# Head-pair groups outermost, K and attention outputs transposed by DMA, half-row score matmuls adjoining, output projection summed per group in SBUF

## The chip, the core and the metric

The kernel runs on one core of one Trainium2 chip. The metric is the device time of one execution in microseconds (us); lower is better. The kernel before took 1077.17 us, the median of 3 runs (1077.12 to 1077.2).

An execution can be profiled. The profile gives the "span" of that one execution, which is about 1.8 us shorter than the time of the same execution (957.5 and 959.26 us in the changed kernel), and for each engine when it was busy and what it waited for. TensorE is named PE (its weight loads PEld), VectorE DVE, ScalarE ACT, GpSimd POOL, and SyncE SP. In the kernels, tiles with `_ps` in their name lie in PSUM, where the results of matmuls are summed; the other tiles lie in SBUF, and DVE or ACT copies from one to the other.

## The reference

A layer norm of x (2048 rows, 640 columns) feeds two branches that are multiplied and added to x. All data is bf16.

```python
xn = layernorm(x)                                   # 2048 x 640
# branch A: 32 heads of 192, only the last W = 512 keys of the cache
q  = (xn @ wq).reshape(2048, 32, 192)
p  = softmax(q @ k_cache[:, -512:].T * 192 ** -0.5)
A  = (p @ v_cache[:, -512:]).reshape(2048, 6144) @ wo
# branch B: a gated feed-forward
B  = (sigmoid(xn @ w_gate) * (xn @ w_up)) @ w_down  # inner width 1536
out = x + A * silu(B)
```

## The kernel before

It has two parts. The feed-forward part (phase B) computes silu(B) for all rows and parks it in memory. The attention part (phase A) takes blocks of 512 rows, `s`, outermost. Inside it goes through the 16 pairs of heads. A head has 192 columns, so a pair has three chunks of 128: one chunk for each head, and one that holds 64 columns of both. The first two give full-row matmuls (all 128 rows of the array contracted), the shared one gives half-row matmuls (64 rows), one head in the upper and one in the lower half.

```python
def stage1(st, hp, pair_idx):            # for each (s, pair)
    # ... loads K, V and wq of the pair again for every s; q projection ...
    for c in range(KC):                  # KC = 4: twelve transposes of K on TensorE
        for i in range(2):
            nc.tensor.transpose(kA_ps[:, i, c * P:(c + 1) * P],
                                kt[:, cb + colA[i]:cb + colA[i] + P], ident[:])
        nc.tensor.transpose(kB_ps[:, c * P:(c + 1) * P],
                            kt[:, cb + KPAD + P:cb + KPAD + 2 * P], ident[:])
    # ... copies kA_ps, kB_ps to kTA (DVE), kTB (ACT) ...

def stage_qk(st, ctxd):
    for c0 in range(0, KC, CG):          # CG = 2
        for c in cs:                     # four full-row matmuls
            for i in range(2):
                nc.tensor.matmul(S_ps[(c, i)][:], lhsT=kA[...], rhs=qA_[:], start=True, stop=False)
        for c in cs:                     # four half-row matmuls
            for i in range(2):
                nc.tensor.matmul(S_ps[(c, i)][:], lhsT=kB[...], rhs=qB_, start=False, stop=True)
        # ... exp on ACT ...

def phase_a2(st):                        # once after all 16 pairs of a block s
    for q in range(TQ):                  # 128 rows
        for fq in range(NG):             # 12 groups of 4 chunks
            for j in range(4):
                nc.tensor.transpose(pT[:, j, :], o_st[q][:, cc * P:(cc + 1) * P], ident[:])
            # copy to oT: DVE on even fq, ACT on odd fq
            for j in range(4):
                for (d0, dsz), oA_ps in zip(d_chunks, oA):
                    nc.tensor.matmul(oA_ps[:], lhsT=oT[:, j, :], rhs=wo_sb[:, cc, d0:d0 + dsz], ...)
        # ... times silu(B), plus x, store ...

for s in range(NST):                     # 4 blocks of rows
    for hp in range(NPAIR):              # 16 pairs
        ...
```

The softmax here doesn't subtract the row's maximum and nothing guards it: scores larger than these inputs give would overflow.

## Time and profile before

| | before |
|---|---|
| time, us (median) | 1077.17 |
| span of the profiled execution, us | 1071.9 |
| TensorE busy | 97% of the span |
| phase B ends (first q matmul of attention) | 177.4 us |
| one step (512 rows, one pair), 64 of them | 9.64 us |
| output phase after 16 steps, 4 of them | about 67.7 us |
| tail after the last matmul | 4.4 us |
| read from memory | 106.04 MB |

First, lines of the profile's page of the kernel before: the span, the busy time and share of each engine, and the chain of work that ended last.

```profile
span 1071.9 us, 19547 instructions
...
PE 1034.7 (97%) x7927; PEld 608.0 (57%) x8048; DVE 439.9 (41%) x1163; ACT 515.0 (48%) x981; POOL 113.9 (11%) x163
...
PE 82%; issue 10%; DMA 3%; ACT 2%; POOL 2%; DVE 1%; POOLq 0%; DVEq 0%
```

TensorE is the limit, and nothing else is near it. So work that leaves TensorE shortens the kernel, and work given to another engine or to the DMA engines costs nothing as long as it stays under TensorE's own time and is done before TensorE needs it.

The next lines are the TensorE timeline of the kernel before, in one step. The columns are start (us), duration (us), engine, line of the kernel, operation with its output and inputs, shape, and count; in brackets, where TensorE was idle before the line, how long and who released it. Matmuls are pipelined, so the distance between two starts is the cost, not the duration.

```profile
251.59 0.28 PE L254 MATMUL kA_ps<-ident,k_sb 128*128 128x128 bf16 x2
251.71 0.22 PE L258 MATMUL kB_ps<-ident,k_sb 128*128 128x128 bf16 x1
...
252.26 0.38 PE L286 MATMUL S_ps<-qT_2577,kTA 128*128 128x512 bf16 x1
...
252.69 0.38 PE L286 MATMUL S_ps<-qT_2577,kTA 128*128 128x512 bf16 x1
252.91 0.38 PE L286 MATMUL S_ps<-qT_2593,kTA 128*128 128x512 bf16 x1
253.22 0.60 PE L293 MATMUL S_ps<-qT_2585,kTB 64*128 64x512 bf16 x4
253.76 0.39 PE L286 MATMUL S_ps<-qT_2577,kTA 128*128 128x512 bf16 x1
...
344.80 0.38 PE L343 MATMUL pTo<-ident,o_st 128*128 128x128 bf16 x4
345.74 0.39 PE L352 MATMUL oA_ps_4061<-wo_sb,oT 128*128 128x512 bf16 x1 [0.56 <-DVE oT L346]
```

Three costs are to be read from it. The twelve K transposes take from 251.59 to 252.26, 0.67 us in each of 64 steps, 0.056 us each. A full-row matmul follows a full-row one after 0.22 us, but the first half-row one comes 0.31 us after the last full one: about 0.1 us more at the switch; and four half-row ones, which run in pairs and would need two times 0.216 us, take 0.54 us (253.22 to 253.76): again 0.1 us more. Two entries and two exits in a step. And the output phase starts with a wait for the copy of its first transposes; such waits for a copy out of PSUM are called bubbles below.

### The profile page before, as it was taken

How to read it: one execution, taken by the hardware profiler on the slowest of the kernel's cores; microseconds unless marked ns; L12 is line 12 of the kernel's file. 1: busy time of each engine (PE TensorE's matmuls, PEld its weight loads, DVE VectorE, ACT ScalarE, POOL GpSimd, SP SyncE). 2: the span in 40 equal slices, each digit the busy share in tenths (PEclk: the TensorE clock that was granted, in tenths of full speed). 3: DMA queues.
4: the chain of work that ended last, by engine and by line, in shares of the span. 5: the costliest groups of instructions: out<-in, count | busy, mean ns of one | idle time of the engine just before them, and what ended most of it. 6: DMA issues, size and time to landing. Idle time of an engine off the chain costs nothing.

```text
span 1071.9 us, 19547 instructions
## 1 busy us (share of the span) xinstructions
PE 1034.7 (97%) x7927; PEld 608.0 (57%) x8048; DVE 439.9 (41%) x1163; ACT 515.0 (48%) x981; POOL 113.9 (11%) x163
## 2 busy tenths in 40 slices
PE   6899999999999999999999999999999999999997
PEld 3445445556556665656556555656566555656664
DVE  4654333444454123544452224544432244544322
ACT  2654223666656114666653235666641165666321
POOL 4211002400010001000010010000000010000000
PEclk9999999999999999999999999999999999999999
DMA  9621002975555013555552024555521054451010
GB/s 303 196 93 50 13 37 77 343 205 130 135 127 163 20 38 78 133 144 131 137 144 65 20 71 127 129 144 132 136 70 38 20 147 127 129 144 50 1 38 13
DMA packets 153578, 115.18 MB, mean 107 GB/s; under 512 B 138000, under 2 KB 140560, under 8 KB 153488
## 3 DMA queue, kind: packets, MB, share of 16 engines
q1 hardware_dynamic: 138048, 53.63, 20.3%
q0 software_dynamic: 15440, 60.30, 18.8%
q8 instruction: 63, 1.03, 0.4%
q14 instruction: 27, 0.22, 0.1%
HBM read 106.04 MB, written 7.86 MB: 106 GB/s over the span
## 4 chain that ended last, share of the span: by engine, by line
PE 82%; issue 10%; DMA 3%; ACT 2%; POOL 2%; DVE 1%; POOLq 0%; DVEq 0%
PE q_ps L236 18%; PE o_ps L315 17%; PE S_ps L286 11%; PE S_ps L293 6%; PE kA_ps L254 3%; ACT oT L348 2%; PE pTo L343 2%; DMA xnT_d<-xnT_sb 1%; PE kB_ps L258 1%; PE g_ps L160 1%; PE u_ps L167 1%; PE oA_ps_4443 L352 1%; PE oA_ps_10299 L352 1%; PE oA_ps_13091 L352 1%; PE oA_ps_7371 L352 1%
## 5 line engine op out<-in xcount | busy, mean ns | idle before, releaser
L236 PE MATMUL q_ps<-xnT_a,wqp 128*128 128x512 bf16 x901 | 214.9, 379 | 5.4 <-DMA wqp<-in_A_wq_dram 2.2
L352 PEld LDWEIGHTS <-oT 128*128 128x128 bf16 x1536 | 115.3, 98 | 102.4 <-DVE oT L346 11.8
L328 DVE TENSOR_SCALAR o_st<-o_ps,rden 128x192 bf16<-128x192 f32 x384 | 148.3, 415 | 9.0
L348 ACT ACTIVATE oT<-pTo 128x512 bf16<-128x512 bf16 x96 | 53.8, 595 | 203.2 <-PE pTo L343 203.2
L236 PEld LDWEIGHTS <-wqp 128*128 128x128 bf16 x960 | 92.4, 97 | 100.8 <-DMA wqp<-in_A_wq_dram 2.7
L321 DVE RECIPROCAL rden<-o_ps 128x2 f32<-128x2 f32 x256 | 41.6, 162 | 192.9 <-PE o_ps L315 192.9
L346 DVE COPY oT<-pTo 128x512 bf16<-128x512 bf16 x96 | 40.7, 424 | 178.5 <-PE pTo L343 177.9
L228 POOL DMA_DIRECT2D wqp<-in_A_wq_dram x64 | 55.9, 874 | 472.5 <-PE q_ps L236 428.2
L326 ACT ACTIVATE o_st<-o_ps,rden 128x192 bf16<-128x192 f32 x128 | 54.0, 422 | 66.1 <-DVE o_st L328 61.2
L286 PEld LDWEIGHTS <-kTA 128*128 128x128 bf16 x512 | 42.1, 97 | 57.4 <-issue 26.7
L265 ACT ACTIVATE kTB<-kB_ps 128x512 bf16<-128x512 bf16 x64 | 38.2, 597 | 70.1 <-PE kB_ps L258 70.1
L160 PE MATMUL g_ps<-xnT_sb,wg_sb 128*128 128x512 bf16 x236 | 62.3, 384 | 1.8 <-DVE xnT_sb L154 1.3
L167 PE MATMUL u_ps<-xnT_sb,wu_sb 128*128 128x512 bf16 x233 | 60.8, 382 | 0.2
L173 ACT ACTIVATE sig_sb<-g_ps 128x512 bf16<-128x512 f32 x48 | 28.1, 597 | 60.9 <-PE g_ps L160 60.4
L174 DVE TENSOR_TENSOR hT_sb<-u_ps,sig_sb 128x512 bf16<-128x512 f32 x48 | 32.9, 690 | 53.8 <-PE u_ps L167 44.4
L343 PE MATMUL pTo<-ident,o_st 128*128 128x128 bf16 x768 | 54.0, 219 | 0.0
L254 PEld LDWEIGHTS <-k_sb 128*128 128x128 bf16 x512 | 42.0, 98 | 15.1
L343 PEld LDWEIGHTS <-o_st 128*128 128x128 bf16 x768 | 45.8, 98 | 7.6
L254 PE MATMUL kA_ps<-ident,k_sb 128*128 128x128 bf16 x512 | 49.7, 219 | 0.0
L258 PE MATMUL kB_ps<-ident,k_sb 128*128 128x128 bf16 x256 | 46.2, 219 | 0.0
L293 PEld LDWEIGHTS <-kTB 64*128 64x128 bf16 x512 | 14.6, 94 | 54.2 <-issue 54.2
L180 PEld LDWEIGHTS <-hT_sb 128*128 128x128 bf16 x384 | 29.8, 98 | 26.7 <-DVE hT_sb L174 3.5
(1006 smaller groups left out, 1839.0 us busy)
## 6 DMA issues: line engine op xcount, KB each, us to landing
wqp<-in_A_wq_dram POOLq DMA_DIRECT2D x64, 480.0 KB, 4.6
k_sb<-in_A_k_cache_dram SPq DMA_DIRECT2D x128, 192.0 KB, 4.8
wo_sb<-in_A_wo_dram POOLq DMA_DIRECT2D x16, 480.0 KB, 9.7
v_sb_96<-in_A_v_cache_dram SPq DMA_DIRECT2D x22, 192.0 KB, 2.9
v_sb_98<-in_A_v_cache_dram SPq DMA_DIRECT2D x22, 192.0 KB, 2.9
v_sb_100<-in_A_v_cache_dram SPq DMA_DIRECT2D x21, 192.0 KB, 2.9
v_sb_102<-in_A_v_cache_dram SPq DMA_DIRECT2D x21, 192.0 KB, 2.9
v_sb_104<-in_A_v_cache_dram SPq DMA_DIRECT2D x21, 192.0 KB, 2.9
```

Of the source, the lines that this page charges most:

```text
L160: nc.tensor.matmul(g_ps[:], lhsT=wg_sb[:, c, f * P:(f + 1) * P], rhs=xnT_sb[:, c * 512:(c + 1) * 512], start=(c == 0), stop=(c == NCD - 1),)
L167: nc.tensor.matmul(u_ps[:], lhsT=wu_sb[:, c, f * P:(f + 1) * P], rhs=xnT_sb[:, c * 512:(c + 1) * 512], start=(c == 0), stop=(c == NCD - 1),)
L236: nc.tensor.matmul(q_ps[:], lhsT=wqp[:, c, j * P:(j + 1) * P], rhs=xnT_sb[:, c * 512:(c + 1) * 512], start=(c == 0), stop=(c == NCD - 1),)
L254: nc.tensor.transpose(kA_ps[:, i, c * P:(c + 1) * P], kt[:, cb + colA[i]:cb + colA[i] + P], ident[:],)
L258: nc.tensor.transpose(kB_ps[:, c * P:(c + 1) * P], kt[:, cb + KPAD + P:cb + KPAD + 2 * P], ident[:],)
L286: nc.tensor.matmul(S_ps[(c, i)][:], lhsT=kA[:, c * P:(c + 1) * P], rhs=qA_[:], start=True, stop=False,)
L293: nc.tensor.matmul(S_ps[(c, i)][:], lhsT=kB[:, c * P:(c + 1) * P], rhs=qB_, start=False, stop=True,)
L315: nc.tensor.matmul(o_ps[:, ii, 0:DH + 1], lhsT=E[i][:, c, q * P:(q + 1) * P], rhs=vt[:, c, 0:DH + 1], start=(c == 0), stop=(c == KC - 1),)
L328: nc.vector.tensor_scalar_mul(dst, o_ps[:, ii, 0:DH], rden[:, ii:ii + 1])
L343: nc.tensor.transpose(pT[:, j, :], o_st[q][:, cc * P:(cc + 1) * P], ident[:])
L348: nc.scalar.activation(oT[:], pT[:], AF.Copy)
L352: nc.tensor.matmul(oA_ps[:], lhsT=oT[:, j, :], rhs=wo_sb[:, cc, d0:d0 + dsz], start=(cc == 0), stop=(cc == NC_O - 1),)
```

## The change

The intent is to take everything but real matmuls off TensorE.

1. Groups of two head pairs are the outermost loop, and the blocks of rows run inside it. K, V and wq of a pair are then loaded and K is transposed once, not once for each of 4 blocks. The output projection of a group is added to a sum in SBUF (f32, by DVE).
2. K and the attention outputs are transposed by the DMA engines, issued on the SP queue: one DMA for each pair (K), one for each step (outputs).
3. The second half of the scores takes the half-row matmuls first, so that all eight half-row matmuls of a step adjoin: two switches in a step where there were four.
4. Phase B transposes only the first 512 rows of xn on TensorE; the rest goes by DMA, once, and stays in SBUF for attention.

The core of the diff, with cuts marked:

```diff
-        for c in range(KC):
-            # [cut] K transposes on TensorE, copies to kTA and kTB
+        kT = kt_pool.tile([P, KC * PC, P], BF16, name="kT")
+        nc.sync.dma_start_transpose(kT[:], k_sb[:].rearrange("p j e d -> p (j e d)"))
 # [cut]
+        u0 = units(range(0, KC // 2))
+        for u in u0:
+            full(*u, True)
+        for u in u0:
+            half(*u, False)
+        exps(u0)
+        u1 = units(range(KC // 2, KC))
+        for u in u1:
+            half(*u, True)
+        for u in u1:
+            full(*u, False)
+        exps(u1)
 # [cut] stage_pv, end:
+        oT = oT_pool.tile([P, TQ * PC, P], BF16, name="oT")
+        nc.sync.dma_start_transpose(oT[:], o_st[:].rearrange("p q d -> p (q d)"))
 # [cut] stage_wo, 12 matmuls for 128 rows of one group, then:
+            if g == 0:
+                nc.vector.tensor_copy(a, oA_ps[:])
+            else:
+                nc.vector.tensor_tensor(a, oA_ps[:], a, ALU.add)
+        if last:
+            nc.vector.tensor_tensor(acc[t][:], acc[t][:], gB_sb[:], ALU.mult)
+            nc.vector.tensor_tensor(o_sb[:], acc[t][:], x_sb[:], ALU.add)
 # [cut] the loop:
+    steps = [(g, s, hp) for g in range(NG) for s in range(NST) for hp in range(g * G, (g + 1) * G)]
+    for k, (g, s, hp) in enumerate(steps):
+        E = stage_s(hp, qT)
+        for _ in range(TQ // G):
+            if wo_queue and wo_queue[0][0] <= k:
+                stage_wo(*wo_queue.pop(0)[1:])
+        qT = stage_q(...)                  # of the next step
+        oT_of[hp] = stage_pv(hp, E)
+        # after a group's last pair: wo_queue.append((k + 2, g, s, oTs, q)) for each 128 rows
 # [cut] phase B:
+                nc.sync.dma_start_transpose(xnT[s][:, :, q * P:(q + 1) * P], xn[:])
```

A transposed output is used no earlier than the second step after its own, so it has a step's time and more to land.

## The prediction

> **What bounds the kernel now.** TensorE. The engine table gives it 1034.7 us busy of a 1071.9 us span (97%), DVE 41%, ACT 48% and a granted clock of 0.999; the chain of waits is 82% TensorE. So only TensorE work and its gaps count. From the timeline: phase B ends at 177.4 us; then 64 pair steps of 9.64 us each (q projection 15 x 0.216 = 3.24, K transposes 12 x 0.055 = 0.66, scores 3.01, PV 2.73), and per 512 rows an output phase of about 67.7 us (16.9 us for each 128 rows).
>
> **What the change removes from TensorE.**
> - 768 K transposes: 64 x 0.66 = 42 us.
> - 768 transposes of attention outputs, 48 x 0.055 = 2.65 us per 128 rows with bubbles around their PSUM copies: 16.9 us shrinks to the matmuls, 48 x (0.216+0.055) = 13.0. Together 16 x 3.9 = 62 us.
> - Score switches. Four full-row matmuls plus four half-row ones should take 0.87 + 0.43 us (halves run in pairs; the trace shows four in 0.54 us) but take 1.50: about 0.1 us at each entry to and exit from half rows. Four such switches per step become two: 0.2 us x 64 = 13 us.
> - Phase B: 60 of 80 x transposes with their copies and the trip of xn through DRAM (about 3 x 1.6 us), the 2.9 us wait for hT, and the 2.2 us wait for wq at the start of A: about 7 to 9 us.
>
> **What it adds.** One DMA transpose of 384 KB per step and one per pair for K, 80 in all, on the SP queue. The trace of before has none, so this is an estimate: at the 261 GB/s that the skill's "DMA: Bandwidth & Descriptors" (section "Latency and other measured facts") gives, 1.5 us plus 2 us fixed. An output is needed two steps later, about 15 us after its issue, and the queue has 9.6 us per transpose, so I expect it hidden. DVE gains 16 f32 additions per 128 rows (0.69 + 0.29 us each group), about 6.3 us per step; ACT about 5.5 us. Both are under the step. The second half of the scores waits for PSUM banks of PV just evicted by DVE: about 1.3 us needed, 1.5 available. The tail is longer: the last rows each need about 2.6 us of DVE, then the store, 11 us after the last matmul against 4.5.
>
> **Sum.** Phase B ends near 171. A step is 3.24 + 2.81 + 2.73 + two output groups of 1.63 = 12.03 us; 64 make 770. Tail 11, start of A 2, small waits 6: span 960, plus the 5 us between span and measured time: about 964 us. Range 945 to 1000. Faster 0.89, same 0.04, slower 0.07.
>
> **What the profile would show.** Right: no K or output transposes on TensorE, step period 12.0 to 12.2 us, TensorE 96% or more, DMA transposes landing in under 10 us, no long TensorE wait for oT or kT; eight half-row matmuls in about 0.97 us. Wrong on switches: eight still with gaps between.
>
> **What would make it wrong.** DMA transposes far slower than the estimate: above 9.6 us each the SP queue becomes the limit and the kernel could be slower than before. In phase B slow transposes hold the four xn buffers, which stall DVE and TensorE. PSUM waits for exp or DVE inside a step, if each reaches 0.5 us, add 30 us.

## The result

| | before | after |
|---|---|---|
| time, us, median (range, runs) | 1077.14 (1075.22 to 1077.2, 4) | 960.89 (959.26 to 963.77, 4) |
| span of the profiled execution, us | 1071.9 | 957.5 |
| TensorE busy | 97% | 97% |
| phase B ends, us | 177.4 | 176.8 |
| one step, us | 9.64 | 12.02 (holds a share of the output projection) |
| attention stage, us | 890.2 | 771.1 |
| tail after the last matmul, us | 4.4 | 9.6 |
| read from memory, MB | 106.04 | 42.07 |

The ratio of the times is 0.8936, 95% interval 0.8916 to 0.8957. Ratios here are the mean time of one kernel's fast runs over the mean of the other's in the same rounds, so not quite the ratio of the medians that are quoted.

"Attention stage" is from the start of the first q matmul to the end of the last matmul, read from the TensorE timeline of the profiled execution. It is the measure that the experiments below lean on, because phase B varied between executions and the attention stage did not.

The page of the changed kernel, the same lines:

```profile
span 957.5 us, 15630 instructions
...
PE 931.4 (97%) x6452; PEld 529.5 (55%) x6452; DVE 464.0 (48%) x1089; ACT 345.5 (36%) x668; POOL 103.1 (11%) x151
...
PE 92%; DMA 6%; DVE 1%; issue 0%; SPq 0%; POOL 0%; ACT 0%; DVEq 0%; POOLq 0%
```

TensorE lost 103 us of busy time (1034.7 to 931.4), and the span lost 114. So the rest of the gain, about 11 us, is idle time that went. The TensorE timeline of the changed kernel:

```profile
501.61 3.40 PE L273 MATMUL q_ps<-xnT_88,wqp 128*128 128x512 bf16 x15
...
513.63 3.40 PE L273 MATMUL q_ps<-xnT_88,wqp 128*128 128x512 bf16 x15
...
520.02 0.38 PE L290 MATMUL S_ps<-qT_5680,kT 128*128 128x512 bf16 x1
520.23 0.38 PE L290 MATMUL S_ps<-qT_5696,kT 128*128 128x512 bf16 x1
520.54 1.04 PE L297 MATMUL S_ps<-qT_5688,kT 64*128 64x512 bf16 x8
521.51 0.39 PE L290 MATMUL S_ps<-qT_5680,kT 128*128 128x512 bf16 x1
```

The step is 513.63 - 501.61 = 12.02 us. The eight half-row matmuls take 0.97 us (520.54 to 521.51), 0.1 us over four times 0.216; the entry still costs the other 0.1 us (0.31 between 520.23 and 520.54). The K and output transposes are gone from TensorE.

One line of the windows view of the changed kernel covers nearly the whole attention stage. Its columns are the stretch, its length, busy us of TensorE, weight loads, DVE, ACT and POOL (each with a count), granted clock (the share of TensorE's full clock that the profile reports), share of the 16 DMA engines, and GB/s. The DMA share adds up the times of all packets; packets can overlap, and it stands above 1 in places (1.32 from 32 to 36 us in this run), so 1.00 is no proof that no more would fit.

```profile
209.90:934.00 724.10, 724.10 (x5243) 423.84 (x5242) 360.99 (x859) 279.96 (x546) 56.97 (x78) 1.00 0.35 74
```

TensorE was busy 724.10 of 724.10 us. Two lines from the DMA view of the changed kernel; the columns are the transfer, the issuing queue, the operation and count, and the median us from issue to landing:

```profile
oT<-o_st SPq DMA_TRANSPOSE x64, 3.7
...
kT<-k_sb SPq DMA_TRANSPOSE x16, 4.1
```

Phase B did not gain. These are TensorE's waits in the kernel before (first fence; phase B only) and in the changed kernel (second fence; whole execution): what waited for what, us in total, times, and the longest.

```profile
PE pT_181 L150 <- DVE xn L141: 9.1, 2, 8.9
PE oB_ps_393 L180 <- DVE hT_sb L174: 2.9, 2, 2.7
PE g_ps L160 <- DVE xnT_sb L154: 1.3, 3, 0.5
```

```profile
PE pT_170 L185 <- DVE xn L172: 8.5, 2, 8.0
PE g_ps L210 <- DVE xnT_86 L190: 5.1, 1, 5.1
PE oB_ps_518 L233 <- DVE hT_sb L222: 1.2, 1, 1.2
PE oA_ps_10848 L354 <- DMA oT<-o_st: 0.8, 1, 0.8
PE u_ps L216 <- DVE hT_sb L222: 0.7, 2, 0.5
PE S_ps L290 <- DVE qT_1672 L281: 0.2, 1, 0.2
```

The waits of before at the later blocks' xnT and at hT are smaller or gone, but there is a new one of 5.1 us at the very start. The DVE timeline of the changed kernel shows why:

```profile
15.21 0.49 DVE L163 BATCH_NORM_STATS2 stats<-x_sb 128x6 f32<-128x320 bf16 x1 [1.21 <-DMA x_sb<-in_A_x_dram]
15.62 0.41 DVE L190 COPY xnT_86<-pT_170 128x512 bf16<-128x512 bf16 x1
15.95 0.41 DVE L190 COPY xnT_86<-pT_172 128x512 bf16<-128x512 bf16 x1
```

DVE ran them in this order. The last transpose that the copies need was done at 11.00 us, but they ran only from 15.62, behind statistics of later rows of x, and those waited for loads that are in flight together with the feed-forward weights (a median of 12.2 us from issue to landing for the 14 x rows on the SP queue). In the kernel's text the copies (L190) come before these statistics (`ln_stats(TQ + f)`, in the loop after them): the order that DVE ran is not the order of the text. It was made when the kernel was built, and only the trace shows it.

### The profile page after: what moved, and what is told of

Its sections match the earlier page's. It is cut to its first block, busy times and chain, and to the rows that moved or that the text cites. A ratio compares the mean times of both kernels' runs of the same rounds, so it can differ in the third digit from the quotient of the medians.

```text
span 957.5 us, 15630 instructions
## 1 busy us (share of the span) xinstructions
PE 931.4 (97%) x6452; PEld 529.5 (55%) x6452; DVE 464.0 (48%) x1089; ACT 345.5 (36%) x668; POOL 103.1 (11%) x151
## 3 DMA queue, kind: packets, MB, share of 16 engines
HBM read 42.07 MB, written 5.24 MB: 49 GB/s over the span
## 4 chain that ended last, share of the span: by engine, by line
PE 92%; DMA 6%; DVE 1%; issue 0%; SPq 0%; POOL 0%; ACT 0%; DVEq 0%; POOLq 0%
PE q_ps L273 22%; PE o_ps L332 18%; PE S_ps L290 12%; PE S_ps L297 6%; PE g_ps L210 4%; PE u_ps L216 4%; DMA x_sb<-in_A_x_dram 3%; DMA xnT_87<-xn 1%; DMA kT<-k_sb 1%; DMA xnT_88<-xn 1%; DMA gB_d<-gB_sb 1%; DMA oT<-o_st 0%; PE oB_ps_1570 L233 0%; PE oB_ps_1536 L233 0%; PE oB_ps_1502 L233 0%
## 5 line engine op out<-in xcount | busy, mean ns | idle before, releaser
L339 DVE TENSOR_TENSOR o_st<-o_ps,rden 128x384 bf16<-128x384 f32 x256 | 142.6, 557 | 8.6
L290 PEld LDWEIGHTS <-kT 128*128 128x128 bf16 x512 | 43.7, 97 | 58.0 <-issue 27.6
L273 PE MATMUL q_ps<-xnT_86,wqp 128*128 128x512 bf16 x240 | 54.4, 379 | 0.0
L273 PE MATMUL q_ps<-xnT_87,wqp 128*128 128x512 bf16 x240 | 54.4, 379 | 0.0
L273 PE MATMUL q_ps<-xnT_89,wqp 128*128 128x512 bf16 x240 | 54.4, 379 | 0.0
L273 PE MATMUL q_ps<-xnT_88,wqp 128*128 128x512 bf16 x240 | 54.4, 379 | 0.0
L297 PEld LDWEIGHTS <-kT 64*128 64x128 bf16 x512 | 19.7, 94 | 42.8 <-issue 27.5
L210 PEld LDWEIGHTS <-wg_sb 128*128 128x128 bf16 x240 | 23.7, 99 | 34.2 <-issue 7.4
L113 POOL DMA_DIRECT2D wqp<-in_A_wq_dram x16 | 13.8, 865 | 265.7 <-PE q_ps L273 264.6
L216 PEld LDWEIGHTS <-wu_sb 128*128 128x128 bf16 x240 | 23.7, 99 | 30.1 <-issue 2.6
L101 POOL DMA_DIRECT2D k_sb<-in_A_k_cache_dram x32 | 24.0, 753 | 117.2 <-DMA kT<-k_sb 100.4
L264 POOL DMA_DIRECT2D wo_g<-in_A_wo_dram x8 | 6.7, 834 | 178.0 <-PE oA_ps_4229 L354 29.4
L210 PE MATMUL g_ps<-xnT_86,wg_sb 128*128 128x512 bf16 x60 | 16.2, 405 | 5.1 <-DVE xnT_86 L190 5.1
L163 DVE BATCH_NORM_STATS2 stats<-x_sb 128x6 f32<-128x320 bf16 x32 | 14.4, 466 | 11.2 <-DMA x_sb<-in_A_x_dram 11.2
## 6 DMA issues: line engine op xcount, KB each, us to landing
x_sb<-in_A_x_dram SPq DMA_DIRECT2D x14, 160.0 KB, 12.2
```

The lines of the kernel that those rows point to most:

```text
L210: nc.tensor.matmul(g_ps[:], lhsT=wg_sb[:, c, f * P:(f + 1) * P], rhs=xnT[s][:, c, :], start=(c == 0), stop=(c == NCD - 1),)
L216: nc.tensor.matmul(u_ps[:], lhsT=wu_sb[:, c, f * P:(f + 1) * P], rhs=xnT[s][:, c, :], start=(c == 0), stop=(c == NCD - 1),)
L273: nc.tensor.matmul(q_ps[:], lhsT=wqp[:, c, j * P:(j + 1) * P], rhs=xnT[s][:, c, :], start=(c == 0), stop=(c == NCD - 1),)
L290: nc.tensor.matmul(S_ps[:], lhsT=kT[:, c * PC + 2 * i, :], rhs=qT[2 * i][:], start=start, stop=not start,)
L297: nc.tensor.matmul(S_ps[:], lhsT=kT[r, c * PC + 1, :], rhs=qT[1][r, :], start=start, stop=not start,)
L339: nc.vector.tensor_tensor(o_st[:, qp * 2:qp * 2 + 2, i * DH:(i + 1) * DH], o_ps[:, :, 0:DH], rden[:].to_broadcast([P, 2, DH]), ALU.mult,)
```

## The experiments

The theory after the first reading: the gain is TensorE work removed, term by term as predicted (switches about 13, K transposes about 42 of which most by loop order, output transposes and their bubbles about 62), and the DMA transposes are hidden with room to spare. The rivals: the loop order or the missing bubbles make the gain and the DMA transposes little of it; or the transposes are hidden only just.

All experiments gave correct results. The last three columns are read from the timeline of one profiled execution.

| run | time, us, median (range) | ratio to before | phase B ends | attention stage | tail |
|---|---|---|---|---|---|
| after, first run | 960.89 (959.26 to 963.77) | 0.8936 | 176.8 | 771.1 | 9.6 |
| a_switch4 | 974.36 (972.96 to 982.62) | 0.9058 | 186.6 | 784.8 | 9.6 |
| b_switch2 | 1061.74 (1060.26 to 1063.77) | 0.9876 | 178.9 | 878.7 | 4.4 |
| a_kT_pe | 986.64 (985.46 to 988.78) | 0.9182 | 194.4 | 783.6 | 9.0 |
| a_kT_pe2 | 968.35 (968.13 to 970.07) | 0.901 | 177.9 | 780.6 | 9.8 |
| a_oT_pe | 1007.88 (1004.27 to 1010.38) | 0.9375 | 182.0 | 817.6 | 8.9 |
| a_both_pe | 1031.7 (1031.34 to 1032.04) | 0.9599 | 190.9 | 829.4 | 9.4 |
| a_transp4x | 975.83 (969.8 to 979.52) | 0.907 | 185.4 | 774.9 | 12.6 |
| a_lag1 | 1012.61 (1009.92 to 1013.13) | 0.941 | 183.5 | 819.3 | 8.6 |
| after_ref (after again) | 961.25 (959.16 to 966.15) | 0.8953 | 178.0 | 771.1 | 9.5 |
| a_start | 962.22 (959.71 to 963.09) | 0.8943 | 177.8 | 771.1 | 9.3 |
| a_tail | 957.95 (957.08 to 963.66) | 0.8918 | 178.7 | 771.0 | 6.4 |
| a_best | 957.5 (953.97 to 959.25) | 0.8904 | 178.0 | 771.0 | 5.6 |

The end of phase B is not a clean number. The profiled execution of a_switch4 took 982.62 us and its four others 972.96 to 976.23, with the same program: 6 to 10 us of phase B come and go. Where a change touches attention alone, its effect is the difference of the attention stage from 771.1 (or from 890.2 for the kernel before); that came out as 771.0 or 771.1 in all five profiles of kernels that have the changed kernel's order of TensorE work in attention (after, after_ref, a_start, a_tail, a_best).

### a_switch4: the half-row matmuls split again

```diff
         for u in u1:
-            half(*u, True)
+            full(*u, True)
         for u in u1:
-            full(*u, False)
+            half(*u, False)
```

> Changed kernel with the second half of the scores put back to full rows first, half rows last, so that a step has four switches between full and half rows and not two. My theory: each switch leaves TensorE about 0.1 us idle and nothing else covers it, so the step goes from 12.02 to 12.22 us and the kernel gets 12.8 us slower (about 974 us). Rival: the switch gap overlaps waits that the step has anyway (PSUM banks that DVE still evicts); then under 4 us slower.

Measured: +13.7 us in the attention stage (784.8 against 771.1), and in time +13.1 us by the ratios ((0.9058 - 0.8936) x 1074.62, the time of before on that chip) or +13.5 by the medians. The theory holds and the rival falls. The profiled execution is this kernel's slowest (982.62), because of phase B: TensorE waited 5.1 us for DVE's gB (until 71.71 us), and the granted clock in the stretch from 45 to 90 us was 0.92. In windows of 5 us (columns as above) it is lowest just after the wait:

```profile
70.00:75.00 5.00, 3.29 (x8) 1.17 (x8) 2.97 (x6) 0.60 (x1) 2.07 (x3) 0.50 1.09 260
75.00:80.00 5.00, 5.00 (x21) 2.17 (x20) 1.38 (x2) 0.95 (x2) 0.68 (x1) 0.85 0.62 121
```

That fits the advice in the Trainium skill, "TensorE: Matmul & The Clock Gate", section "Why this matters for your kernels", to leave TensorE no idle gap over about 3 us; here a gap of 5.1 us is followed by a lower clock. After the gap of 2.7 us in the kernel before (until 44.13 us) the clock stayed at 1.00.

### b_switch2: the kernel before with adjoining half-row matmuls, nothing else

```diff
-            for c in cs:                    # all full-row
-                ...
-            for c in cs:                    # all half-row
-                ...
+            for part in ((0, 1) if c0 == 0 else (1, 0)):
+                first = part == (0 if c0 == 0 else 1)
+                for c in cs:
+                    ...                     # full-row if part == 0, else half-row
```

> Kernel before with one part of the change alone: the second half of the scores takes its half-row matmuls first, so that the eight adjoin and two of four switches go. My theory: 0.2 us for each of 64 steps, so 12.8 us faster than before, ratio 0.988. Rival: in the old order of PSUM banks the half rows would wait for banks that DVE and ACT still evict, and the gain is under 4 us.

Measured: 0.9876 of before, interval 0.9853 to 0.9899 (clear of 1), and the attention stage 11.5 us shorter (890.2 to 878.7). TensorE's timeline of this run shows the eight half-row matmuls in one piece, with the same 0.97 us as in the changed kernel:

```profile
254.01 1.03 PE L289 MATMUL S_ps<-qT,kTA 128*128 128x512 bf16 x4
254.97 1.04 PE L289 MATMUL S_ps<-qT,kTB 64*128 64x512 bf16 x8
255.94 1.04 PE L289 MATMUL S_ps<-qT,kTA 128*128 128x512 bf16 x4
```

So this term stands on its own, done alone and undone alone: 11.5 to 13.7 us, or about 0.2 us in each of 64 steps. It is the cheapest part of the change, an order of eight instructions.

### a_kT_pe and a_kT_pe2: K transposed on TensorE once for each pair

```diff
+    def pe_transpose(dst, src):
+        # twelve nc.tensor.transpose into two PSUM tiles, one copied by DVE, one by ACT
...
-        nc.sync.dma_start_transpose(kT[:], k_sb[:].rearrange("p j e d -> p (j e d)"))
+        pe_transpose(kT, k_of[hp][:].rearrange("p j e d -> p (j e d)"))
```

> Changed kernel, but K transposed on TensorE once per pair of heads (192 transposes of 128x128, copies on DVE and ACT), output transposes left to DMA. My theory: K's part of the gain came mostly from the loop order, which cuts the transposes from 768 to 192; what DMA adds for K is 192 x 0.055 = 10.6 us. So 10 to 13 us slower (971 to 974 us). Rival, the reading in my prediction that moving K to DMA is worth 42 us: about 40 us slower.

Measured: +26 us. Neither number fits. The attention stage has +12.5 (783.6), as the theory says, but phase B ended at 194.4, 17.6 us later than in the changed kernel. From the timeline of a_kT_pe (all engines), the long DMA transposes on the SP queue, the DVE instruction that waited for one, and TensorE:

```profile
34.69 27.84 SPq L212 DMA_TRANSPOSE xnT<-xn  x10
...
51.50 0.45 DVE L184 TENSOR_SCALAR xn<-x_sb,mv,rstd 128x640 bf16<-128x640 bf16 x1 [14.42 <-DMA xnT<-xn]
...
57.85 2.29 PE L228 MATMUL u_ps<-xnT,wu_sb 128*128 128x512 bf16 x5 [15.79 <-DVE hT_sb L234]
```

In the changed kernel the gpsimd queue waits for a DMA transpose of K (19.3 us, until 51.3 us) before it issues the next loads:

```profile
51.32 0.77 POOL L101 DMA_DIRECT2D k_sb<-in_A_k_cache_dram  x1 [19.33 <-DMA kT<-k_sb]
```

With K on TensorE that brake is gone: between 32.4 and 36.9 us it issued six more loads of V and wq, just when the first xn transposes were issued (34.69). The slowest xn transpose took 19.4 us to land, where the median is 2.6. DVE had no free xn buffer, and TensorE waited 15.8 us for DVE. To keep this out, a second run leaves the first group's K on the DMA engines and puts only the later 14 pairs on TensorE.

> Again K on TensorE in the changed kernel, but the first two pairs stay on DMA, so that the loads of phase B keep the changed kernel's order (the run before this one had a 15.8 us wait of TensorE there: transposes of xn took 14 us beside loads of K, V and wq). My theory: the 26 us of that run are 10 to 13 us of TensorE transposes and the rest that collision in phase B; without it 168 x 0.055 = 9.2 us, up to 12 us, slower than the changed kernel (970 to 973 us). Rival: K transposes on TensorE cost more inside the attention steps than their own time, and it stays at 985 us.

Measured: +8 us in time by the ratios ((0.901 - 0.8936) x 1074.72), +9.5 us in the attention stage, phase B ends at 177.9, no long wait. The theory holds. 168 transposes in 9.5 us are 0.057 us each, close to what the kernel before showed (0.056). So moving K to DMA is worth about 10 us; the larger part of the 42 us comes from the loop order, which needs 192 transposes instead of 768.

### a_oT_pe and a_both_pe: attention outputs on TensorE; and both

```diff
-        nc.sync.dma_start_transpose(oT[:], o_st[:].rearrange("p q d -> p (q d)"))
+        pe_transpose(oT, o_st[:].rearrange("p q d -> p (q d)"))   # one step later, behind the scores
```

> Changed kernel, but attention outputs transposed on TensorE in the next step after its scores (12 per step, copies on DVE and ACT), K left to DMA. My theory: only the transposes' own 64 x 0.66 = 42 us come back, because the copies now hide behind other matmuls: 42 to 46 us slower (1003 to 1007 us). Rival: the bubbles around the copies that the kernel before shows (about 1.3 us per 128 rows, 20 us in all) belong to TensorE transposes as such: about 62 us slower.

Measured: +47 us in time ((0.9375 - 0.8936) x 1074.62), and +46.5 us in the attention stage. Of the difference in time some is phase B (a 2.9 us wait for gB in the profile). The rival said that the bubbles of the old output phase come back with the transposes; they do not: in the attention stage the profile has no wait of TensorE for a copy of a transpose, only 2.1 us in three waits for o_st near the end. That the step's other work between a transpose and its use is the reason is an inference from the order of the step.

> Changed kernel with both kinds of transposes on TensorE: only the new loop order, the adjoining half rows and the sum in SBUF are left of the change. My theory: the costs add, 53 to 59 us slower than the changed kernel (1014 to 1020 us), so that more than half of the whole gain of 116 us does not need DMA transposes. Rival: DMA transposes carry most of the gain, 1040 us or more.

Measured: 1031.7 us, +71, more than expected, and less than the rival's 1040. Phase B ended at 190.9 with the collision of a_kT_pe; the attention stage is 829.4, +58.3, where the two parts alone gave 12.5 + 46.5 = 59.0. They add. So with no DMA transpose in the attention stage at all, 890.2 - 829.4 = 60.8 of its 119.1 us of gain remain. This is the answer to the first rival: about half is left without the DMA transposes (the loop order, the adjoining half rows and the bubbles together), and about half is theirs.

### a_transp4x: each output transposed four times

```diff
         nc.sync.dma_start_transpose(oT[:], o_st[:].rearrange("p q d -> p (q d)"))
+        for _ in range(3):
+            spare = spare_pool.tile([P, TQ * PC, P], BF16, name="spare")
+            nc.sync.dma_start_transpose(spare[:], o_st[:].rearrange("p q d -> p (q d)"))
```

> Changed kernel, but each attention output is transposed by DMA four times, three of them into a spare tile, so the SP queue carries 272 transposes of 384 KB and not 80. My theory: a transpose occupies the queue for about 1.5 to 3.7 us of a 12 us step and is needed 15 us later, so four in a step still fit and the time stays within 3 us of the changed kernel (about 961 us). Rival: the transposes are near their limit and set the pace when they grow: then three more at 3.7 us make the step 15 us or more and the kernel 1150 us.

Measured: +15 us in time; neither number. But the attention stage has only +3.8 us; 3.0 are in a longer tail (12.6), where the spare transposes stand in the last transposes' way, and the rest is phase B (8.6 us in the profiled execution), which the edit does not touch. The windows view of this run (columns as above):

```profile
210.00:930.00 720.00, 717.08 (x5192) 419.69 (x5190) 355.00 (x848) 276.01 (x538) 54.76 (x74) 1.00 1.00 171
```

TensorE nearly keeps its pace, at a DMA share of 1.00. The 3.8 us are waits for oT: 4.2 us in three, the longest 2.2, and one oT took 13.3 us to land. So four transposes in a step are hidden all but these waits; five were not run. The shares also size one transpose. The same stretch of a_oT_pe, which has no output transposes:

```profile
210.00:930.00 720.00, 720.00 (x5624) 437.37 (x5623) 368.70 (x851) 290.98 (x571) 48.31 (x62) 1.00 0.14 36
```

The share is 0.14 there and 0.35 in the changed kernel. 0.21 of a 12.02 us step is 2.5 us of packet time on all 16 engines for 384 KB, about 156 GB/s (an estimate worked out from these two shares).

### a_lag1: the output projection one step earlier

```diff
-                wo_queue.append((k + 2, g, s, oTs, q))
+                wo_queue.append((k + 1, g, s, oTs, q))
```

> Changed kernel, but the output projection of a group starts one step earlier, right after the next step's scores. My theory: what hides the DMA transpose is the lag. The second output of a group is then needed 3.6 us after its last PV matmul and is ready after about 0.9 us of DVE, 3.7 us of DMA and semaphores, 4.9 us; so TensorE waits about 1.3 us in every second step and the kernel is about 40 us slower (1000 us). Rival: the transpose is fast enough, and the lag is not needed: within 5 us of 961.

Measured: +52 us in time and +48.2 us in the attention stage, against an expected +40. The waits for oT add up to 40.6 us in 32 waits, as expected. From TensorE's waits and its timeline in this run:

```profile
PE oA_ps L354 <- DMA oT<-o_st: 40.6, 32, 3.5
```

```profile
513.66 0.98 PE L354 MATMUL oA_ps<-wo_g,oT 128*128 128x512 bf16 x6
515.53 2.62 PE L354 MATMUL oA_ps<-wo_g,oT 128*128 128x512 bf16 x18 [0.89 <-DMA oT<-o_st]
```

The rest of the 48 is mostly the way of counting. The profile counts idle time from a matmul's modelled end. By starts, the lines shown lose 1.06 us and not 0.89 (the step is 13.08 us instead of 12.02); 0.17 more in each of 32 waits makes 46 of the 48.2 (an estimate).

So a transpose of 3.7 us is free only because the order gives it more than 3.7 us. A step earlier, and 40% of the gain is lost (48.2 of 119.1).

### after_ref, a_start, a_tail, a_best: the two ends

What is left in the changed kernel is at the ends: waits in phase B, and a tail of 9.6 us. Four kernels on one chip, five rounds each.

> The changed kernel itself, as the reference of this chip for the three that follow. 958 to 963 us, ratio to before 0.892 to 0.896. If its span holds a wait in the feed-forward part that the first profile did not have (the oB and gB waits of 3 to 5 us that several variants showed), that wait belongs to the chip and not to the variants.

Measured: 961.25 us, ratio 0.8953 (interval 0.8924 to 0.8982); attention stage 771.1 again. No long gB wait in this profile (0.6 us). The variants that have one (a_switch4 5.1 us, a_oT_pe 2.9, a_transp4x 5.5, a_lag1 4.1) leave the text of phase B alone, and two of them ran on this chip. So by the expectation's own test, on one profile, the wait does not belong to the chip. In a_switch4 it belongs to single executions, as the other times show; what makes it in the others stays open.

a_start orders the loads and the layer norm of phase B:

```diff
-        for t in range(TQ, NST * TQ):
-            load_x(t, nc.sync)
+        # x rows of block 1 behind the gate and up weights, the rest behind w_down, all on gpsimd
...
-                if s == 0 and TQ + f < NST * TQ:
-                    ln_stats(TQ + f)
-            if s == 0:
-                ln_rest()
+                if s + 1 < NST and 4 <= f < 4 + TQ:
+                    ln_stats((s + 1) * TQ + f - 4)
+                if s + 1 < NST and f == 8:
+                    ln_next(s + 1)
+            if s in (1, 2):                 # K, V, wq of the first two groups only now
+                for hp in range((s - 1) * G, s * G):
+                    load_pair(hp, gate=hT_sb)
```

> Changes only the first 177 us: later x rows loaded behind the gate and up weights, layer norm of a block done one block ahead instead of all at once, K, V and wq of the first two groups loaded only after the second and third block's gate and up matmuls. Theory: the feed-forward part took 6 us more than predicted because the vector engine stood in order behind statistics of x rows that had not landed (5.1 us wait of the tensor engine at 16 us) and behind the transposes of xn (0.5 + 0.2 + 1.2 us). These go: attention starts at 169 to 172 us instead of 176.8, total about 6 us less, 952 to 956, ratio to the changed kernel 0.991 to 0.996. Rival: the 5 us are the weight loads themselves arriving late, the wait is only renamed: attention starts at 175 to 177 and the time stays within 1.5 us.

Measured: no gain (0.8943 against 0.8953, phase B ends at 177.8). My theory that 6 us go falls as stated, and so does the rival's reason, though its number for the time (within 1.5 us) came true. The waits that it aimed at are gone: the first gate matmul starts at 10.85 us, 5.2 us earlier, and TensorE does not wait for xnT or hT. But two waits took their place. TensorE's waits in a_start between 45 and 180 us, and then DVE's longest single wait:

```profile
PE u_ps L221 <- DVE gB_sb L250: 6.3, 2, 4.2
```

```profile
DVE gB_sb L250 <- DMA gB_d<-gB_sb: 25.6, 2, 13.9
```

Ten loads of K, V and wq now stand on the gpsimd queue directly ahead of two writes of gB (78.7 to 87.5 us), with two transposes of that K in flight too (landing after up to 13.8 us). One such write landed after 12.9 us, where the median is 2.5; the two gB buffers were full, DVE stood 13.9 us, and TensorE 4.2 of them. The granted clock was 0.96 in 90 to 135 us and again in 135 to 180. So the edit that took the first wait away made the second. Whether more gB buffers, or another queue for the gB writes, would keep the 5 us was not run.

a_tail forms the sum of the earlier groups times silu(B), plus x, ahead on POOL in the last group:

```diff
+    def prepare(t):                        # in the last group, a step ahead
+        # ... loads of gB and x ...
+        nc.gpsimd.tensor_tensor(acc[t][:], acc[t][:], gB_sb[:], ALU.mult)
+        nc.gpsimd.tensor_tensor(acc[t][:], acc[t][:], x_sb[:], ALU.add)
...
+            for (d0, dsz), oA_ps in zip(d_chunks, oA):
+                nc.vector.tensor_tensor(o_sb[:, d0:d0 + dsz], oA_ps[:], gB_t[t][:, d0:d0 + dsz], ALU.mult)
+            nc.vector.tensor_tensor(o_sb[:], o_sb[:], acc[t][:], ALU.add)
```

> Changes only the last group: the gate product and the residual of the sum of the earlier groups are formed ahead on the gpsimd engine, so that after the last matmuls a 128-row block needs two multiplications out of PSUM and one addition (about 1.8 us by the durations of the profile, 2.6 before). Theory: the vector engine bounds the 10 us tail after the last matmul (6.8 us of it before its last instruction), so 2.5 to 3.5 us less, 957 to 958. Rival: the output write to memory bounds it, or the gpsimd work slows the vector engine in the last group: no gain, or more than 1 us lost.

Measured: 957.95 us, 3.3 us under the changed kernel's median on that chip, and the tail 6.4 us instead of 9.5. The size is as expected, and the profile shows it where it was expected. The intervals of the two ratios overlap (0.889 to 0.8945 and 0.8924 to 0.8982), so the times alone would not prove it.

> Both. If the two parts are independent, the gains add: about 9 us less than the changed kernel, 949 to 954, ratio to before 0.882 to 0.888. If it gives less than the better of the two parts alone, they share something that the traces did not show.

Measured: 957.5 us, ratio 0.8904 (0.8881 to 0.8927), not the 949 to 954 expected. Its tail is 5.6 us, its phase B ends at 178.0, with the gB waits of a_start (6.2 us in two). It is the lowest of all runs, 3.75 us under the changed kernel on that chip, with intervals that just overlap; a_tail alone gives nearly all of it.

## Why the prediction was right

964 us were predicted and 960.89 measured, inside the range of 945 to 1000. Term by term, with the profiled execution of the changed kernel:

| term | predicted, us | measured, us |
|---|---|---|
| phase B ends | 171 | 176.8 |
| 64 steps | 770 | 771.1, which includes the next two rows |
| start of attention | 2 | 0.25 |
| small waits | 6 | 0.8, one wait for the last oT |
| tail | 11 | 9.6 |
| from span to time | 5 | 1.8 in the same execution (959.26 - 957.5); the median is another 1.6 above it |

The mechanism was right. TensorE bounded the kernel and still does; the step was predicted as 12.03 us and is 12.02. What left TensorE left the time. The 117 us that were expected for attention (42 + 62 + 13) are 119.1, and the experiments give this split of them:

- Score switches: predicted 13, measured 13.7 undone and 11.5 done alone. The Trainium skill, "TensorEngine Tiling (Array Packing)", section "Key Properties", states that changing the tiling mode drains TensorE. The runs agree with a cost at each change, of about 0.1 us for an entry and 0.1 us for an exit (0.31 us instead of 0.22 between the starts, and 0.97 instead of 0.86 for eight half-row matmuls); that a drain makes it is the page's statement and was not tested apart.
- K transposes: predicted 42 as one sum (before, 768 at 0.056 are 43). Measured 9.5 for 168 of them (a_kT_pe2) and 12.5 for all 192 (a_kT_pe), for the DMA; the loop order's part is an estimate, 576 x 0.056 = 32.
- Output transposes with bubbles: predicted 62 as one sum. Measured 46.5 for the transposes themselves (a_oT_pe, 2.1 of it waits). What remains of 119.1 after 13.7, 12.5, 46.5 and 32 is about 14, of which 2.2 are the old wait for wq (at 190.48 us), and the rest falls to the bubbles by subtraction. The trace of before sizes them more directly: its four output phases take 270 us between TensorE's starts, of which 768 transposes at 0.056 are 43 and 768 pairs of matmuls at 0.272 are 209; about 19 are left (an estimate). Subtraction gives less because the parts cost a little more to put back than they took before (46.5 against 43, 12.5 against 11, 13.7 against 12.8). No run takes the bubbles away alone.
- DMA transposes hidden: right. Predicted 1.5 us plus 2 us each, from the rate in the Trainium skill ("DMA: Bandwidth & Descriptors", section "Latency and other measured facts"); measured 3.7 us to landing. a_transp4x shows the room (four in a step are hidden but for 4.2 us in all) and a_lag1 what it costs to have none.

Where the text was wrong, the errors cancelled:

- "Phase B: ... about 7 to 9 us", and so "Phase B ends near 171". It gained 0.5 us. The removed waits and transposes are gone, as said, but the first gate matmul starts at 16.08 us and not at 11.76, because DVE ran the copies of xnT behind statistics of x rows that had not landed. I had counted what the change removes there, and not that in the built kernel later rows' work would run before it on DVE. a_start shows that these 5 us can be taken away, and also that on that queue they come back elsewhere. The 2.2 us wait for wq that I put at the start of attention was 13 us later in the trace of before (190.48 us); attention began without a wait.
- "Small waits 6". There were none in the steps (724.10 us busy of 724.10), and 0.8 us at the end. The PSUM waits of 0.1 us a step that this allowed for did not appear.
- "the 5 us between span and measured time". That difference took the span of one execution of before and the median time of others (1077.17 - 1071.9). Within one execution it is 1.8 us.

6 us too little in phase B, against 7 us too much at the start of attention and in small waits and 3 us too much between span and time, make the sum look better than its parts. That the total came out within 3 us is in part luck; the 12.02 us of the step are not.

## What to carry to other kernels

When one engine is busy for 97% of the span, price every instruction on it by start-to-start distance in the timeline; such a sum predicted a step to 0.01 us, and adding the parts' effects was exact to 1 us. A DMA transpose was free here only with a use far enough behind it: give it a step, and test how many fit in that time. At a start-up, list from the trace, not from the kernel's text, what each engine and queue runs ahead of the first thing that the bounding engine needs: here a statistic placed there cost in full, and moving the loads did not help, because writes at their new place waited on the same queue.

## What the Trainium skill lacked or had wrong

- "TensorEngine Tiling (Array Packing)", section "Key Properties", says that a change of tiling mode drains TensorE and gives no size. Here an entry to and an exit from half-row matmuls cost about 0.2 us together, 11.5 to 13.7 us over 64 steps, which is the whole gain of adjoining them.
- "DMA: Bandwidth & Descriptors", section "Latency and other measured facts", gives 261 GB/s for a DMA transpose with a non-contiguous middle dimension, and "Advanced Engine Details and Errata", section "X-Bar Transpose (TRN2)", 350 to 400 GB/s, as fast as other DMAs. One transpose's 3.7 us to landing agrees with the first figure plus the fixed 2 us of the same section. The packet time of the engines comes out longer than either: about 2.5 us for 384 KB, some 156 GB/s (an estimate from two DMA shares), and with four in a step the 16 engines were at a share of 1.00 with 171 GB/s. As packets can overlap, this is not shown to be a ceiling.
- No page gives a number for DMA transposes with loads beside them. In a_kT_pe, from 44 to 56 us, with xn transposes (0.54 MB moved) and the last loads (0.59 MB) in flight, the 16 engines moved 92 to 96 GB/s at a share of about 1.2, where they had moved 277 to 290 GB/s just before (28 to 40 us); one xn transpose landed after 19.4 us (median 2.6). In a_start a 160 KB write behind ten loads landed after 12.9 us (median 2.5).
- "VectorE: DVE Perf Modes", section "The three transpose paths", compares 390 ns on TensorE with 1309 ns by DMA for one 128x128 block. These are times of one block alone and do not price a stream: here TensorE took 0.056 us each from start to start (0.061 with the waits, 46.5 us for 768), and a DMA of 12 such blocks took 3.7 us to landing, of which 2.5 us of packet time (the estimate above).
